# Issuing fifteen of sixteen V-tile loads from ScalarE's DMA queue instead of the sync queue, in a one-token attention and MLP kernel

## The chip, the cores and the metric

One core of one Trainium2 chip. The metric is the device time of one execution in microseconds (us); the profile's span is about 1.8 us shorter. Names: PE is the matmul engine, DVE VectorE, ACT ScalarE, POOL GpSimd, SP SyncE. A "queue" is the DMA queue of the engine that issues a load; "landing" is the moment at which a load's completion is seen.

## The reference, cut to what matters

```python
# B=4, one new token, D=576, 32 query heads, 16 KV heads, head size 128, last W=2048 of 8192 positions
xn = layernorm(A_x)
q  = xn @ wq
p  = softmax(q . K[:, :, -W:] / sqrt(128));  o = p . V[:, :, -W:]
out = A_x + o @ wo + B(xn)          # B: a small mixer and an MLP with w3 (576x4608) and w4 (4608x576)
```

For one token, all of the work is reading: per KV head one K tile and one V tile of 2.10 MB, 32 tiles in all, and 20 MB of weights.

## The kernel before

Six buffers are shared by K and V tiles. All loads are issued by SyncE in one list, and so they stand in one queue:

```python
def load_kv(kind, h):
    win = k_win if kind == "K" else v_win
    t = kvp.tile([P, NC, Dh], BF16, tag="kv", name=f"{kind.lower()}n")     # kvp: 6 buffers
    nc.sync.dma_start(out=t[:].rearrange("p c d -> p (c d)"), in_=...)

order = [("K", 0), ("K", 1), ("K", 2)]
for h in range(Hkv):
    order.append(("V", h))
    if h + 3 < Hkv:
        order.append(("K", h + 3))
# wo goes in ahead of V0, V4, V8, V12; w3 behind V2; w4 last
```

The end of the list is therefore: K14, wo3, V12, K15, V13, V14, V15, w4.

## Time and profile before

| | before |
|---|---|
| time, median | 212.0 us |
| PE / DVE / ACT busy | 70% / 57% / 16% |
| bytes read | 87.17 MB, 415 GB/s over the span |
| DMA engines busy with the sync queue | 97.5% |

Three rows from the page of the kernel before: the mean busy share of the DMA engines in 40 slices of the span (9 is 90% or more), the rate in each slice, and the sync queue's packets, MB and share.

```profile
DMA  7999999999999999999999999999999999999991
GB/s 281 418 399 430 421 430 435 427 430 436 436 442 414 426 433 420 446 424 433 436 421 433 430 420 437 433 433 422 433 426 430 422 442 433 421 436 426 421 414 60
q1 hardware_dynamic: 6640, 87.17, 97.5%
```

The loads run without a gap up to the last slice.

```profile
kn<-in_A_k_cache_dram SPq DMA_DIRECT2D x1, 2048.0 KB, 24.1
...
w_sb<-in_B_w_dram SPq DMA_DIRECT2D x1, 144.0 KB, 22.2
```

K15 landed at 155.98 + 24.1 = 180.1 us, the last byte of all loads at 184.9 + 22.2 = 207.1 us, and the span ended at 210.2, 3.1 us after it.

### The profile page before, as it was taken

How to read it: one execution, taken by the hardware profiler on the slowest of the kernel's cores; microseconds unless marked ns; L12 is line 12 of the kernel's file. 1: busy time of each engine (PE TensorE's matmuls, PEld its weight loads, DVE VectorE, ACT ScalarE, POOL GpSimd, SP SyncE). 2: the span in 40 equal slices, each digit the busy share in tenths (PEclk: the TensorE clock that was granted, in tenths of full speed). 3: DMA queues.
4: the chain of work that ended last, by engine and by line, in shares of the span. 5: the costliest groups of instructions: out<-in, count | busy, mean ns of one | idle time of the engine just before them, and what ended most of it. 6: DMA issues, size and time to landing. Idle time of an engine off the chain costs nothing.

```text
span 210.2 us, 2389 instructions
## 1 busy us (share of the span) xinstructions
PE 147.2 (70%) x941; PEld 62.4 (30%) x955; DVE 120.1 (57%) x217; ACT 33.9 (16%) x64; POOL 2.8 (1%) x15
## 2 busy tenths in 40 slices
PE   0395694789394008849699689997883956988954
PEld 0132231224131002314154234343431321543533
DVE  4832999267831082637603879898578381593220
ACT  7603100021111000202012211220211020202300
POOL 4010000000000000000000000000000000000000
PEclk9998599589979555979699969999999695899999
DMA  7999999999999999999999999999999999999991
GB/s 281 418 399 430 421 430 435 427 430 436 436 442 414 426 433 420 446 424 433 436 421 433 430 420 437 433 433 422 433 426 430 422 442 433 421 436 426 421 414 60
DMA packets 6659, 87.32 MB, mean 415 GB/s; under 512 B 748, under 2 KB 1016, under 8 KB 1400
## 3 DMA queue, kind: packets, MB, share of 16 engines
q1 hardware_dynamic: 6640, 87.17, 97.5%
q8 instruction: 7, 0.11, 0.2%
q14 instruction: 4, 0.03, 0.0%
q10 hardware_dynamic: 8, 0.00, 0.0%
HBM read 87.17 MB, written 0.00 MB: 415 GB/s over the span
## 4 chain that ended last, share of the span: by engine, by line
DMA 65%; PE 22%; DVE 8%; issue 2%; ACT 1%; SPq 1%; DVEq 0%
DMA w_sb<-in_B_w_dram 33%; DMA vn<-in_A_v_cache_dram 26%; PE S L338 9%; DMA wq_sb<-in_A_wq_dram 6%; DVE kt L225 4%; PE O L390 3%; PE g_ps L456 2%; PE acc L183 2%; PE q_ps L285 2%; PE oT L403 1%; DVE mx L344 1%; PE S L360 1%; DVE qz L317 1%; PE gT_ps L468 1%; ACT q_sb L296 1%
## 5 line engine op out<-in xcount | busy, mean ns | idle before, releaser
L225 DVE STREAM_TRANSPOSE kt<-kn 128x1024 int32<-128x1024 int32 x64 | 76.3, 1216 | 11.1 <-DMA kn<-in_A_k_cache_dram 10.8
L338 PE MATMUL S<-kt,qz 128*128 128x512 bf16 x242 | 76.1, 437 | 5.2 <-DVE kt L225 3.1
L390 PE MATMUL O<-vn,PT 128*32 128x512 bf16 x256 | 27.9, 434 | 38.7 <-DMA vn<-in_A_v_cache_dram 37.5
L338 PEld LDWEIGHTS <-qz 128*128 128x128 bf16 x256 | 21.8, 104 | 42.0 <-issue 26.2
L366 ACT ACTIVATE E<-S 128x512 bf16<-128x512 f32 x16 | 9.5, 597 | 119.8 <-PE S L360 119.8
L390 PEld LDWEIGHTS <-PT 128*32 128x32 bf16 x256 | 7.3, 95 | 47.0 <-DVE kt L225 25.2
L372 DVE STREAM_TRANSPOSE PT<-E 128x512 bf16<-128x512 bf16 x16 | 11.4, 710 | 15.1 <-ACT E L366 15.1
L356 DVE TENSOR_REDUCE nm<-mg 8x1 bf16<-8x16 f32 x16 | 2.3, 146 | 23.0 <-PE mg L351 22.9
L397 ACT ACTIVATE O_sb<-O,rd 128x512 f32<-128x512 f32 x16 | 11.0, 686 | 16.2 <-issue 11.0
L344 DVE TENSOR_REDUCE mx<-S 128x1 f32<-128x512 f32 x16 | 10.5, 657 | 1.3 <-PE S L338 1.3
L413 DVE TENSOR_REDUCE on<-oT 128x8 bf16<-128x128 f32 x16 | 4.5, 280 | 11.1 <-PE oT L403 11.1
L403 PE MATMUL oT<-ident_w,O_sb 128*128 128x128 f32 x64 | 10.6, 291 | 0.2 <-issue 0.2
L403 PEld LDWEIGHTS oT<-ident_w,O_sb 128*128 128x128 f32 x64 | 8.6, 153 | 4.6 <-issue 2.4
L183 PE MATMUL acc<-wo_sb,op 128*8 128x288 bf16 x56 | 7.5, 286 | 0.0
L376 PEld LDWEIGHTS dn<-rs,same_j 128*128 128x128 f32 x32 | 5.8, 188 | 2.9 <-ACT E L366 0.7
L360 PE MATMUL S<-nm,j_row 8*128 8x512 bf16 x16 | 6.6, 410 | 0.0
L183 PE MATMUL acc<-w_sb,gT 128*8 128x288 bf16 x38 | 5.1, 286 | 1.9 <-DMA w_sb<-in_B_w_dram 1.9
L329 PE MATMUL S<-negbig,ohT 4*128 4x512 bf16 x16 | 6.2, 385 | 0.2 <-issue 0.2
L351 PE MATMUL mg<-dm,sel_jb 128*8 128x16 bf16 x16 | 2.8, 174 | 4.0 <-DVE dm L346 3.5
L183 PEld LDWEIGHTS <-op 128*8 128x8 bf16 x64 | 4.6, 87 | 2.4 <-issue 0.3
L456 PE MATMUL g_ps<-w_sb,ln2T 128*32 128x512 bf16 (+1 forms) x50 | 5.3, 480 | 0.0
L351 PEld LDWEIGHTS <-sel_jb 128*8 128x8 bf16 x16 | 1.3, 83 | 12.7 <-issue 6.8
(93 smaller groups left out, 80.0 us busy)
## 6 DMA issues: line engine op xcount, KB each, us to landing
kn<-in_A_k_cache_dram SPq DMA_DIRECT2D x16, 2048.0 KB, 22.3
vn<-in_A_v_cache_dram SPq DMA_DIRECT2D x16, 2048.0 KB, 24.8
wo_sb<-in_A_wo_dram SPq DMA_DIRECT2D x4, 1152.0 KB, 25.5
w_sb<-in_B_w_dram SPq DMA_DIRECT2D x1, 4608.0 KB, 35.8
wq_sb<-in_A_wq_dram SPq DMA_DIRECT2D x1, 4096.0 KB, 12.4
w_sb<-in_B_w_dram SPq DMA_DIRECT2D x1, 1728.0 KB, 33.6
w_sb<-in_B_w_dram SPq DMA_DIRECT2D x1, 1440.0 KB, 27.8
w_sb<-in_B_w_dram SPq DMA_DIRECT2D x2, 576.0 KB, 33.8
```

The lines of the kernel that those rows point to most:

```text
L183: nc.tensor.matmul(out=to[q:q + OR, :], lhsT=lhsT[:, NI - 1 - i:NI - 1 - i + OR], rhs=rhs[:, i * CW:(i + 1) * CW], start=start, stop=False ...
L225: nc.vector.transpose(out=kt[:], in_=src)
L329: nc.tensor.matmul(out=S_ps[h][:].rearrange("p (c k) -> p c k", k=QD), lhsT=ohT[:], rhs=negbig[:].unsqueeze(1).to_broadcast([B, SC, QD]), ...
L338: nc.tensor.matmul(out=S_ps[h][:], lhsT=qz[:, z0:z0 + P], rhs=kt[:, ib, :, e:2 * QD:2].rearrange("p c k -> p (c k)"), start=False, stop=Fa ...
L344: nc.vector.reduce_max(out=mx[:], in_=S_ps[h][:], axis=AX.X)
L360: nc.tensor.matmul(out=S_ps[h][:], lhsT=j_row[:], rhs=st.pop(("nm", h))[:, 0:1].to_broadcast([NJ, NW]), start=False, stop=False, skip_grou ...
L366: nc.scalar.activation(out=E[h][:].rearrange("p c k -> p (c k)"), in_=S_ps.pop(h)[:], func=ACT.Exp, scale=scale, accum_out=rs[:])
L372: nc.vector.transpose(out=PT[h][:], in_=E.pop(h)[:])
L390: nc.tensor.matmul(out=O_ps[h][g * QD:(g + 1) * QD], lhsT=PT[h][:, c, :], rhs=vn[:, :, c, :], start=(s == 0), stop=False, skip_group_check ...
L397: nc.scalar.activation(out=O_sb[h][:], in_=O_ps.pop(h)[:], func=ACT.Copy, scale=st.pop(("rd", h))[:, 0:1])
L403: nc.tensor.transpose(out=oT[:, s, :], in_=o[:, s, :], identity=ident_w[:, s * NJ:s * NJ + P])
L456: nc.tensor.matmul(out=g_ps[g * QD:(g + 1) * QD], lhsT=ln2T[:, k, :], rhs=rhs, start=(j == 0), stop=False, skip_group_check=True)
```

## The change

The intent is to spread the issue of the loads over two engines and to let K and V proceed independently of each other.

```diff
     def load_kv(kind, h):
-        nc.sync.dma_start(out=t[:].rearrange("p c d -> p (c d)"),
+        eng = nc.scalar if kind == "V" and h < Hkv - 1 else nc.sync
+        eng.dma_start(out=t[:].rearrange("p c d -> p (c d)"),
                           in_=win[:, h].rearrange("b (p c) d -> p b (c d)", c=NC))
```

## The prediction

> **What bounds the kernel now.** The loads. In the 40-slice view the DMA row reads 9 from slice 1 to 38; the queue table gives the sync queue 97.5% of the 16 engines' span and 87.17 MB. Between the first issue (0.73 us) and the landing of the last w4 piece (205.0 us, chain of waits) that is 0.427 MB/us. PE is 70% busy, DVE 57%, ACT 16%. The chain is 65% DMA. The tail after the last landing is 5 us.
>
> **What the change does.** No byte is added or removed. Fifteen of sixteen V loads (31 MB) move from the sync stream to ScalarE's:
>
> 1. Fifteen issues of 0.54 us (timeline) enter ACT's stream: 8 us on an engine with 34 us of work. ACT's load of V(t+1) waits for the last PV matmul of V(t-2); the next ACT instruction, the scaling of that head's output, needs the same matmul. So almost no new blocking. One exception: completion semaphores are shared, eight for both streams in program order, and V5's load waits for w3's landing. ACT stands still there, but the next K tile (K5) lies behind w3 anyway.
> 2. V0 and V1 can be issued only after ACT's copies into qz, near 22 us (before: 4.3 and 13.1). The sync queue holds wq, K0 to K3 and wo0, 14 MB or 33 us of transfer, so the DMA engines do not run dry.
> 3. Two queues are active together. The Trainium skill, "DMA: Bandwidth & Descriptors", section "Issuing engines are not separate DMA queues", says that loads started by different engines run on the same 16 engines and interleave. So the sum of the rates stays 0.427 MB/us; only the order of landing changes. V runs ahead up to its three buffers; w3, wo and K tiles behind them land later (estimate: w3 at 75 to 80 us instead of 68.4, K5 at 80 to 87).
>
> **How much is on the critical path.** Total transfer, unchanged. A DMA bubble needs every issued load to have landed, and then compute would be the limit; an undisturbed head takes about 7 us (ACT timeline, Exp to Exp, 124.7 to 131.7 to 138.5) against 4.19 MB / 0.427 = 9.8 us of loads per head, so compute catches up after the late w3. The tail: V15 stays on the sync queue ahead of w4, so w4 is still last. If V13 and V14 lag on ACT's queue they share with w4; compute has some 4 us of slack there (the last head's PV ends at 197.8, its projection work near 202, last landing 205), so a loss of 0 to 3 us is possible. Possible gain: at most the idle 1 to 2% of the DMA engines.
>
> **Predicted time:** 212.3 us, 8 in 10 between 210.2 and 215.2. Faster by over 2%: 0.04; within 2%: 0.84; slower by over 2%: 0.12.
>
> **What would show it right or wrong.** Queue table: about 31.5 MB on ScalarE's queue, 55.7 on the sync queue, shares summing to about 97%. Mean rate 411 to 419 GB/s, DMA row 9 from slice 1 to 38. Last w4 landing 203 to 208 us, tail near 5 us. ACT timeline: V0 issue near 22 us, Exp of head 4 at or after 85 us, the mlp at 103 to 118 us.
>
> **What would make it wrong.** Two interleaved streams running at another total rate than one (each 1% is 2 us); ACT held at a V load while PE needs its next result, so that buffers come free late and the DMA row shows a gap; V14 landing behind w4 and stretching the tail.

## More of the kernel before

The step of head t does this on the engines, in program order:

```python
for t in range(Hkv):
    for s in range(4):
        k_transpose(...)       # DVE: slice s+1 of K_t; at s == 3 the first slice of K_(t+1)
        ...                    # softmax of head t-1: Exp on ACT at s == 2
        pv(t - 2, s)           # PE: P x V of head t-2
        k_scores(t, s)         # PE: scores of head t
    flush_loads()              # issue the loads whose buffers this step has freed
```

So step 14 needs V12, the end of step 14 needs K15, and step 15 needs V13. V14, V15 and w4 come after that.

The timeline of the kernel before, 180 to 196 us (start, duration, engine, line, operation; in brackets the idle time before it and what ended it):

```profile
182.45 2.33 DVE L225 STREAM_TRANSPOSE kt<-kn 128x1024 int32<-128x1024 int32 x2
184.92 0.40 PE L390 MATMUL O<-vn,PT 128*32 128x512 bf16 x4 [0.63 <-DMA vn<-in_A_v_cache_dram]
190.59 0.60 ACT L366 ACTIVATE E<-S 128x512 bf16<-128x512 f32 x1 [7.02 <-PE S L360]
195.22 0.60 ACT L366 ACTIVATE E<-S 128x512 bf16<-128x512 f32 x1 [2.17 <-PE S L360]
```

DVE transposes K15 without having waited for it. PE waits 0.63 us for V13, at 184.92. The last two lines are the Exp of heads 14 and 15. For two loads, the issue from the timeline and the time to landing from the DMA view of a window around it: K15, and the last piece of w4.

```profile
155.98 0.54 SPq L103 DMA_DIRECT2D kn<-in_A_k_cache_dram  x1
184.90 0.33 SPq L141 DMA_DIRECT2D w_sb<-in_B_w_dram  x1
```

## The result, and the profile after

The changed kernel takes 217.04 us (216.47 to 217.85, six runs) against 212.0 (211.9 to 212.22, six runs). The ratio is 1.0242, with a 95% interval of 1.0216 to 1.0267: slower by 2.4%.

The same rows from the page of the changed kernel; q10 is ScalarE's queue.

```profile
DMA  8999999999999999999999999999999999999910
GB/s 286 394 422 431 434 430 419 433 437 428 469 431 421 407 427 437 421 431 434 437 425 431 427 422 439 428 434 431 428 426 434 428 433 426 434 425 426 400 45 1
q1 hardware_dynamic: 4480, 55.71, 60.8%
q10 hardware_dynamic: 2168, 31.46, 34.1%
```

There is still no gap and the rate is the same. The last load is not later at all; the two slices at the end (5.4 us each) hold almost no transfer. The timeline of the changed kernel from 180 to 204 us shows what happens instead:

```profile
189.88 2.37 DVE L226 STREAM_TRANSPOSE kt<-kn 128x1024 int32<-128x1024 int32 x2 [8.77 <-DMA kn<-in_A_k_cache_dram]
191.18 1.87 PE L339 MATMUL S<-kt,qz 128*128 128x512 bf16 x4 [7.96 <-DVE kt L226]
198.44 0.60 ACT L367 ACTIVATE E<-S 128x512 bf16<-128x512 f32 x1 [16.29 <-PE S L361]
203.08 0.60 ACT L367 ACTIVATE E<-S 128x512 bf16<-128x512 f32 x1 [2.17 <-PE S L361]
```

DVE now waits 8.77 us for K15, PE waits 7.96 us for DVE, and the last Exp begins at 203.08 instead of 195.22. Issue and time to landing of K15 and of the last two pieces of w4 in the changed kernel:

```profile
162.40 0.54 SPq L104 DMA_DIRECT2D kn<-in_A_k_cache_dram  x1
189.87 0.80 SPq L142 DMA_DIRECT2D w_sb<-in_B_w_dram  x2
```

```profile
kn<-in_A_k_cache_dram SPq DMA_DIRECT2D x1, 2048.0 KB, 27.5
...
w_sb<-in_B_w_dram SPq DMA_DIRECT2D x2, 144.0 KB, 16.9
```

K15 lands at 189.9, 9.8 us later than before; the last byte lands at about 207, as before. So the same bytes arrive in the same time, but in another order. The size of the delay can be checked. At 0.43 MB/us (429 to 431 GB/s in windows from 120 to 170 us of both traces), the bytes that land behind K15 were V13, V14, V15 and w4 before: 3 x 2.10 + 5.31 = 11.6 MB, or 27.0 us, which puts K15 at 207.1 - 27.0 = 180.1 (measured 180.1). In the changed kernel only V15 and w4 land behind it, 7.4 MB or 17.2 us, which puts it near 189.9 (measured 189.9). ScalarE's queue, whose last tile is V14, moved 0.02 MB from 188.5 to 189.0 us and next to nothing after that, so V14 was in just ahead of K15. K15 was also issued 6.4 us later than before (162.40 against 155.98), but that did not hold it: K14, ahead of it in the same queue, was taken up only at 173.55.

How the second queue gets ahead is visible in one microsecond, 162 to 163 us, of the changed kernel's DMA view (packets, MB, share of 16 engines):

```profile
q1 hardware_dynamic: 15, 0.23, 53.5%
q10 hardware_dynamic: 14, 0.21, 49.7%
```

In this microsecond each queue gets about half of the rate. The Trainium skill, "DMA: Bandwidth & Descriptors", section "Queues, rings and completion order", says that each DMA engine takes turns between the queues that have work, packet by packet; the 15 and 14 packets here agree with that. A V tile on its own queue then no longer stands behind the K tiles and weights that were issued before it.

### The profile page after: what moved, and what is told of

It is laid out like the page before. It is cut to its first block, busy times and chain, and to the rows that moved or that the text cites. A ratio compares the mean times of both kernels' runs of the same rounds, so it can differ in the third digit from the quotient of the medians.

```text
span 216.0 us, 2388 instructions
## 1 busy us (share of the span) xinstructions
PE 145.9 (68%) x941; PEld 62.6 (29%) x955; DVE 119.7 (55%) x217; ACT 34.0 (16%) x64; POOL 2.7 (1%) x15
## 3 DMA queue, kind: packets, MB, share of 16 engines
q1 hardware_dynamic: 4480, 55.71, 60.8%
q10 hardware_dynamic: 2168, 31.46, 34.1%
HBM read 87.17 MB, written 0.00 MB: 404 GB/s over the span
## 4 chain that ended last, share of the span: by engine, by line
DMA 57%; PE 24%; DVE 13%; issue 3%; ACT 1%; DVEq 0%; ACTq 0%
DMA kn<-in_A_k_cache_dram 45%; DVE kt L226 8%; DMA vn<-in_A_v_cache_dram 7%; PE S L339 6%; PE acc L184 6%; DMA wq_sb<-in_A_wq_dram 6%; PE O L391 3%; PE oT L404 2%; PE g_ps L457 2%; DVE mx L345 2%; PE q_ps L286 2%; PE S L361 1%; DVE dm L347 1%; DVE qz L318 1%; PE gT_ps L469 1%
## 5 line engine op out<-in xcount | busy, mean ns | idle before, releaser
L339 PE MATMUL S<-kt,qz 128*128 128x512 bf16 x242 | 74.7, 431 | 45.1 <-DVE kt L226 43.6
L391 PE MATMUL O<-vn,PT 128*32 128x512 bf16 x256 | 26.3, 411 | 4.9 <-DMA vn<-in_A_v_cache_dram 4.7
L391 PEld LDWEIGHTS <-PT 128*32 128x32 bf16 x256 | 6.8, 94 | 14.1 <-issue 12.9
L184 PE MATMUL acc<-wo_sb,op 128*8 128x288 bf16 x56 | 8.8, 318 | 0.0
L475 DVE COPY g_x<-gT_ps 128x64 f32<-128x64 f32 (+1 forms) x3 | 0.6, 195 | 7.4 <-PE gT_ps L469 7.4
```

The lines of the kernel that those rows point to most:

```text
L184: nc.tensor.matmul(out=to[q:q + OR, :], lhsT=lhsT[:, NI - 1 - i:NI - 1 - i + OR], rhs=rhs[:, i * CW:(i + 1) * CW], start=start, stop=False ...
L339: nc.tensor.matmul(out=S_ps[h][:], lhsT=qz[:, z0:z0 + P], rhs=kt[:, ib, :, e:2 * QD:2].rearrange("p c k -> p (c k)"), start=False, stop=Fa ...
L391: nc.tensor.matmul(out=O_ps[h][g * QD:(g + 1) * QD], lhsT=PT[h][:, c, :], rhs=vn[:, :, c, :], start=(s == 0), stop=False, skip_group_check ...
```

## The experiments

Theory A: order. K15 lands late because V tiles overtake it, and a stretch of compute that follows K15 can no longer be hidden behind the remaining loads. Theory B: ACT is held by its V loads. Its stream did stand still once for 11.1 us, for w3's landing, ahead of V5's load; Exp of head 4 began at 94.5 us instead of 85.4. Theory C: two queues move bytes more slowly. The last landing near 207 us in both kernels already speaks against C.

### V13 and V14 back on the sync queue

```diff
-        eng = nc.scalar if kind == "V" and h < Hkv - 1 else nc.sync
+        eng = nc.scalar if kind == "V" and h < Hkv - 3 else nc.sync
```

> The changed kernel with V13 and V14 back on the sync queue, behind K15. Theory A (order: K15, the last K tile, lands 10 us later because V tiles on the second queue overtake it, and a compute tail of about 26 us starts at its landing): with V13, V14, V15 and w4 all behind K15, K15 lands at 180 to 184 us instead of 189.9 and the time goes back to 211.5 to 213.5 us. Theory B (ACT is held by its V loads and gives its results late): 13 of 15 loads are still on ACT, w3's wait included, so most of the loss stays, 215.5 us or more. Theory C (two queues move bytes slower): the last landing stays at 205 us in both, no change, 216 to 217 us.

Measured: 212.26 us, ratio to the kernel before 1.0008 (0.9991 to 1.0025). DVE gets K15 at 180.22, as this line of its timeline shows. The loss is gone with 13 of 15 V loads still on ACT.

```profile
180.22 2.37 DVE L226 STREAM_TRANSPOSE kt<-kn 128x1024 int32<-128x1024 int32 x2 [1.30 <-DMA kn<-in_A_k_cache_dram]
```

### One queue, K15 moved behind V14

```diff
+    order.remove(("K", Hkv - 1))
+    order.insert(order.index(("V", Hkv - 1)), ("K", Hkv - 1))
```

(in the kernel before, after the list is built)

> The kernel before, one queue, nothing on ACT, with K15 moved in the load order from ahead of V13 to behind V14. Theory A: K15 lands at 187 to 191 us instead of 180.1, the last load still at 205 us, and the time is 215 to 218 us. Theories B and C: there is one queue and no load on ACT, so 212 us.

Measured: 217.86 us, ratio 1.0276 (1.0255 to 1.0296). Its timeline:

```profile
189.75 2.37 DVE L225 STREAM_TRANSPOSE kt<-kn 128x1024 int32<-128x1024 int32 x2 [7.58 <-DMA kn<-in_A_k_cache_dram]
198.94 0.60 ACT L366 ACTIVATE E<-S 128x512 bf16<-128x512 f32 x1 [15.74 <-PE S L360]
203.58 0.60 ACT L366 ACTIVATE E<-S 128x512 bf16<-128x512 f32 x1 [2.17 <-PE S L360]
```

One queue, no load on ACT, and nearly the same picture as in the changed kernel: the order alone makes the loss. Theories B and C don't explain this run.

### The same V tiles on GpSimd's queue

```diff
-        eng = nc.scalar if kind == "V" and h < Hkv - 1 else nc.sync
+        eng = nc.gpsimd if kind == "V" and h < Hkv - 1 else nc.sync
```

> The changed kernel with the same V tiles issued by GpSimd in place of ScalarE: still two queues that overtake each other, but ACT holds no load and waits for none. Theory A: as slow as the change or slower, 215 to 220 us, K15 landing at 187 us or later. Theory B: back to 211 to 213 us. Descriptors are made by software here, so a rate of its own is possible; the queue table and the last landing tell that apart.

Measured: 218.49 us, ratio 1.0295 (1.0258 to 1.0332). The first line is from its timeline, the second from its queue table (GpSimd's queue):

```profile
189.58 2.37 DVE L226 STREAM_TRANSPOSE kt<-kn 128x1024 int32<-128x1024 int32 x2 [9.77 <-DMA kn<-in_A_k_cache_dram]
...
q0 software_dynamic: 2160, 31.46, 34.0%
```

DVE gets K15 at 189.58, after a wait of 9.77 us. ACT issues no V load and waits for none, and the loss remains. Theory B has fallen. The queue has no rate of its own that shows: 430 GB/s from 120 to 170 us, and the last landing near 207 us as before.

### The mirror image: K4 to K15 on ScalarE's queue

```diff
-        eng = nc.scalar if kind == "V" and h < Hkv - 1 else nc.sync
+        eng = nc.scalar if kind == "K" and h > 3 else nc.sync
```

> The mirror image: K4 to K15 on ScalarE's queue, V and the weights on the sync queue. Again two queues and 12 loads in ACT's stream. Theory A: K tiles are now the ones that overtake, K15 lands at 165 to 180 us, V15 and w4 stay last, and the time is 211 to 213.5 us. Theory B: ACT is held at its loads again, slower by about as much, 215 us or more. Theory C: 215 us or more.

Measured: 214.02 us, ratio 1.0098 (1.0078 to 1.0118), just above what theory A expected and below theories B and C. K15 landed at 180.4 us, 0.4 past the range forecast. But now V12 was the late one, as this line of its timeline shows (step 14 needs V12):

```profile
180.63 0.62 PE L391 MATMUL O<-vn,PT 128*32 128x512 bf16 x4 [9.02 <-DMA vn<-in_A_v_cache_dram]
```

So K15 is not the only tile that counts. V13, behind V12 in the same queue, landed at 185.2 us, and nothing waited for it.

### Only V13 and V14 on ScalarE's queue

```diff
-        eng = nc.scalar if kind == "V" and h < Hkv - 1 else nc.sync
+        eng = nc.scalar if kind == "V" and Hkv - 3 <= h < Hkv - 1 else nc.sync
```

> Only V13 and V14 on ScalarE's queue, the other 14 V tiles back on the sync queue: the complement of the first run. Theory A: these two tiles alone overtake K14, wo3, V12 and K15, so K15 lands at 187 to 191 us and nearly the whole loss is there, 215.5 to 218.5 us. Theory B (ACT held by its loads): 2 of 15 loads are left, and w3's wait is not, so 212 to 213 us.

Measured: 219.96 us, ratio 1.0372 (1.0356 to 1.0387): two loads on the second queue cost more than fifteen, and more than was expected. Two things were off. V12 is back on the sync queue here, and V13, which is needed a step later, overtakes it:

```profile
185.04 0.62 PE L391 MATMUL O<-vn,PT 128*32 128x512 bf16 x4 [13.99 <-DMA vn<-in_A_v_cache_dram]
```

The wait for V12 is 14 us. K15 landed at 157.31 + 32.5 = 189.8 us, as forecast and later than V12, but DVE did not wait for it, since the late step 14 came to it only at 191.3. And from the last Exp to the end it took 14.7 us instead of the 12.9 of the changed kernel; the granted PE clock in that stretch was 0.88 against 0.99. Why the clock differed there was not pursued.

### K15 on ScalarE's queue too, ahead of V13

```diff
-        eng = nc.scalar if kind == "V" and h < Hkv - 1 else nc.sync
+        eng = nc.scalar if (kind == "V" and h < Hkv - 1) or (kind == "K" and h == Hkv - 1) else nc.sync
```

> The changed kernel with one more tile on ScalarE's queue: K15, which in that stream stands behind V12 and ahead of V13. All 15 V loads stay on ACT. Theory A: V13 and V14 can no longer overtake K15, it lands at 178 to 183 us and the time is 211.5 to 213.5 us. Theory B: one load more on ACT, so 217 us or more.

Measured: 218.01 us, ratio 1.0283 (1.0253 to 1.0312). The landing of K15 came as theory A forecast, the time did not; the time is what theory B named (217 or more), but the wait is for a V tile and not on ACT. Two lines of its timeline say why:

```profile
181.84 2.37 DVE L226 STREAM_TRANSPOSE kt<-kn 128x1024 int32<-128x1024 int32 x2 [2.91 <-DMA kn<-in_A_k_cache_dram]
...
190.99 0.62 PE L391 MATMUL O<-vn,PT 128*32 128x512 bf16 x4 [10.29 <-DMA vn<-in_A_v_cache_dram]
```

K15 is there at 181.8, but V13, now behind K15 on ScalarE's queue, lands only at 190.9, because V15 and w4 on the sync queue overtake it. Theory A as first stated (K15) has fallen. Mended, it reads: what counts is the last to land of all the tiles that steps 14 and 15 need, V12, K15 and V13; every byte that lands ahead of it but is needed only later (V14, V15, w4) is time lost. The table of all runs corrects this once more.

### One queue, K15 moved one place only

```diff
-    order.insert(order.index(("V", Hkv - 1)), ("K", Hkv - 1))
+    order.insert(order.index(("V", Hkv - 2)), ("K", Hkv - 1))
```

(against the run with K15 behind V14)

> Half the dose on one queue: the kernel before with K15 moved one place, from ahead of V13 to behind it. Theory A with the sizes read so far: K15 lands at 184 to 186 us instead of 180.1. In the slow kernels the last Exp began 13 us after K15's landing and the span ended 12.9 us after that Exp; before, it ended at 210.2 by the loads. So the last Exp begins near 198 us and the span ends near 211 us: 0.5 to 1.5 us more than before, 212.4 to 213.5 us, not half of the 5.9 us that two places cost. If the cost grew evenly with K15's delay it would be 214.5 to 215.5 us.

Measured: 213.39 us, ratio 1.0062 (1.0050 to 1.0075), span 211.0 us; K15 was taken up at 185.21 and the last Exp began at 198.08. All four numbers are as forecast (the profiled run is the fastest of the five; the others' spans are 211.5 to 211.7). Half the delay costs only a quarter of the time (1.4 us against 5.9), since the first part of it falls into slack.

### One queue, V13 and V14 exchanged

```diff
+    order.remove(("V", Hkv - 3))
+    order.insert(order.index(("V", Hkv - 1)), ("V", Hkv - 3))
```

> Theory A mended after the run with K15 on ACT: what counts is the last to land of the tiles that the final two heads' steps need, V12, K15 and V13, whatever the queue. Here one queue as before, K15 untouched in its place, only V13 and V14 exchanged. Mended theory: K15 still lands at 180 us, V13 at 189 to 190 instead of 184.9; the last Exp begins 10 to 12 us after that, at 200 to 202, the span ends near 213 to 215 us, and the time is 214.5 to 216.5 us. The theory as first stated (K15 alone): 212 us.

Measured: 216.5 us, ratio 1.0215 (1.0197 to 1.0232): slower beyond doubt, though whether by more than 2% the interval leaves open. The mended theory's numbers held to within 0.1 us: PE gets V13 at 189.84, the last Exp begins at 202.09, and the span ends at 215.1.

```profile
189.84 0.62 PE L390 MATMUL O<-vn,PT 128*32 128x512 bf16 x4 [5.32 <-DMA vn<-in_A_v_cache_dram]
190.39 1.89 PE L338 MATMUL S<-kt,qz 128*128 128x512 bf16 x4
...
202.09 0.60 ACT L366 ACTIVATE E<-S 128x512 bf16<-128x512 f32 x1 [2.17 <-PE S L360]
```

Not a single K tile has moved here.

### V14 alone back on the sync queue

```diff
-        eng = nc.scalar if kind == "V" and h < Hkv - 1 else nc.sync
+        eng = nc.scalar if kind == "V" and h < Hkv - 2 else nc.sync
```

> The changed kernel with V14 alone back on the sync queue, behind K15; V0 to V13 stay on ACT. Mended theory: of what landed ahead of K15 in the changed kernel only V14 is needed after it (V13 is needed in the same step), so moving V14 behind it lets the later of K15 and V13 land at 184 to 186 us instead of 189.9; the last Exp begins near 198 us, the span ends near 211 us, time 212 to 213.5 us: one tile of fifteen is nearly the whole loss. Theory B (ACT held): 14 of 15 loads left, 216.5 us or more.

Measured: 212.35 us, ratio 1.0038 (0.9994 to 1.0082; three runs of 212.05 to 212.56 and one of 214.22). K15 was taken up at 185.02, and the span of the profiled run is 210.2, that of the kernel before. One tile of fifteen, V14, is nearly the whole loss.

```profile
185.02 2.37 DVE L226 STREAM_TRANSPOSE kt<-kn 128x1024 int32<-128x1024 int32 x2 [2.96 <-DMA kn<-in_A_k_cache_dram]
...
197.31 0.60 ACT L367 ACTIVATE E<-S 128x512 bf16<-128x512 f32 x1 [2.17 <-PE S L361]
```

### All runs in one table

Times in us from the profiled runs. "Last waited for" is the tile of V12, K15, V13 whose arrival ended the last wait ahead of the last Exp.

| kernel | queues | last waited for, taken up at | last Exp begins | span ends |
|---|---|---|---|---|
| before | one | V13, 184.9 | 195.2 | 210.2 |
| change | two | K15, 189.9 | 203.1 | 216.0 |
| V13, V14 on sync | two | V13, 185.0 | 198.0 | 210.9 |
| K15 behind V14 | one | K15, 189.8 | 203.6 | 216.5 |
| V on GpSimd | two | K15, 189.6 | 203.1 | 216.5 |
| K on ACT | two | V12, 180.6 | 199.5 | 212.4 |
| only V13, V14 on ACT | two | V12, 185.0 | 203.5 | 218.2 |
| K15 on ACT too | two | V13, 191.0 | 202.5 | 217.0 |
| K15 behind V13 | one | K15, 185.2 | 198.1 | 211.0 |
| V13 behind V14 | one | V13, 189.8 | 202.1 | 215.1 |
| V14 on sync | two | K15, 185.0 | 197.3 | 210.2 |

The table corrects the mended theory. Not the last of the three to land decides, but each landing plus the compute between it and the last Exp, and the largest sum counts. From arrival to the last Exp it took 18.5 to 18.9 us for V12, 12.3 to 13.8 for K15 and 10.3 to 13.0 for V13. That is how V12 at 180.6 led to a later last Exp (199.5) than V13 at 184.9 did (195.2).

These stretches of compute are not constant. Before, and with V13 and V14 on the sync queue, PE gets V13 at 184.92 and 185.03, and yet the last Exp begins at 195.22 and 197.96. In the first PE had waited 0.63 us and its granted clock from 185 to 191 us was 1.00; in the second it had waited 4.35 us and the clock was 0.50. The four score matmuls that follow, before and then with the two tiles on the sync queue:

```profile
185.26 1.08 PE L338 MATMUL S<-kt,qz 128*128 128x512 bf16 x4
...
185.59 1.89 PE L339 MATMUL S<-kt,qz 128*128 128x512 bf16 x4
```

So the long wait was followed by a slow start, and cost more here than its own length. The change moved the last arrival by 5.0 us (184.9 to 189.9) and the last Exp by 7.9; a slower start of PE of the size seen here, 2.7 us, would be nearly the rest (an estimate from these two runs).

In every kernel the last load landed near 207 us: the windows of the eleven traces show 14 to 42 GB/s from 206.5 to 207.0 us and nothing from 207 to 208. The end of the span follows two limits: the last landing plus about 3 us (210.2), and the last Exp plus 12.9 to 13.4 us (14.5 and 14.7 in the two runs with a granted clock of 0.88 in that stretch). Before, the first limit held: the last Exp plus 12.9 would have been 208.1, so there were 2.1 us of slack. The change moved the last Exp by 7.9 us; 7.9 - 2.1 = 5.8 us, which is the difference of the spans, 216.0 - 210.2.

No run beat the kernel before. With the rate of the loads the same in one queue and in two, no order of loads can end before the last landing at 207 us; the best two-queue version, with V13 and V14 on the sync queue, equals it.

## Why the prediction was right or wrong

It was wrong: 212.3 us was predicted, with 215.2 as the upper end, and 217.04 was measured. "Within 2%" had been given 0.84.

- **Bound by the loads, and the total transfer is unchanged: right.** 87.17 MB, 31.46 MB on ScalarE's queue and 55.71 on the sync queue as forecast, no gap, and the last landing stayed near 207 us. The prediction named 205.0 as the last landing. That was w4's third piece of six, read off the chain of waits; the last piece landed at 207.1, so the tail is 3 us and not 5. The shares sum to 94.9% rather than 97% only because the span grew. But the end of the changed kernel is no longer bound by the loads: 9 us of work follow the last landing, where 5 had been forecast.
- **"The sum of the rates stays 0.427 MB/us": right.** It rested on the Trainium skill, "DMA: Bandwidth & Descriptors", section "Issuing engines are not separate DMA queues", and the trace agrees: 431 and 429 GB/s in the windows from 120 to 140 and from 140 to 170 us before, 430 and 429 after. (The 0.427 itself was taken up to 205.0 us, ahead of the last landing.)
- **ACT's stream: right.** V0 was issued at 21.75 us. ACT stood 11.1 us for w3 at V5's load and it cost nothing in the end: K5, behind w3, came even later, and the Exp of head 7 began at 126.3 us instead of 124.7, that of head 13 at 179.7 instead of 181.1. The runs with V on GpSimd and with only two tiles on ACT show that the loss does not come from there.
- **"w3, wo and K tiles behind them land later": right.** w3 landed at 76.1 us, K5 at 88.5, a little past the 80 to 87 of the estimate. But this was applied to the middle of the kernel alone, where compute catches up.
- **"If V13 and V14 lag on ACT's queue they share with w4; compute has some 4 us of slack there, so a loss of 0 to 3 us": the step that failed.** It looked for late V tiles. V13 and V14 were early, and in V14 that was the harm: it passed K15, so the last of K15 and V13 landed at 189.9 instead of 184.9. The prediction's own sentence about K tiles behind the weights and V's head start was not carried to the last heads, where nothing is left to catch up in. And the slack was measured at the wrong place: from the last PV matmul to the last landing, instead of along the chain from K15 to the end of the span. Along that chain, it was 2.1 us at the last Exp, while the last Exp moved by 7.9.
- **Not counted at all: a late operand costs its wait, and then a slower start as well.** The Trainium skill, "TensorE: Matmul & The Clock Gate", section "What's actually happening", says that after an idle window of about 3.4 us the array's clock drops to half. That agrees with the trace: four score matmuls took 1.87 us right after the 8 us wait for K15, and 1.08 us around 181 us; the granted clock was 0.56 from 190 to 196 us and 1.00 from 180 to 183.

## What to carry to other kernels

When loads bind, a single queue in the order of need is itself a schedule. In this case a second queue added no bandwidth (429 to 431 GB/s either way), but took about half of it for whatever stood first there, and so let bytes that were needed later land ahead of bytes that were needed first. Before splitting a load list over queues, look at the last operands with a long compute chain behind them, count the bytes that land behind each of them before and after, and compare that with the chain's length to the end; in the middle of this kernel such delays were made up (Exp of head 4 was 9.1 us late, that of head 13 was not), at the end they were not. If two queues are wanted all the same, let the last few tiles, and the weights behind them, stand in one queue, in order of need: here one tile (V14) made the difference between 2.4% slower and equal.

## What the Trainium skill lacked or had wrong

- "DMA: Bandwidth & Descriptors", section "Rules for kernel authors", says that spreading DMAs over SP, ACT and GpSimd "doesn't help". The rate was indeed the same, but the page does not say that it can harm through the order of landing: 2.4% slower here with fifteen tiles on a second queue, 3.7% with two, and 1.0% with the K tiles there. It has the turn-taking that explains it, in "Queues, rings and completion order", without this consequence.
- Same page: it calls the time to initiate a DMA "usually small" and says that semaphore waits happen on the issuing sequencer, but gives no case of what this costs an engine that also computes. Here it was 0.54 us per 2 MB load in ACT's stream, and once 11.1 us of standing still, because the load waited for another queue's load (w3) in this program's shared completion semaphores.
